# One decode step, attention beside a gated MLP: the MLP's output weights are dealt out anew over the DMA engines, and two products keep their weight loads

## The chip, the core and the metric

The kernel runs on one core of a Trainium2 chip. The metric is the device time of one execution in microseconds (us); the median over several runs is compared. Before the change it is 663.55 us, the median of three runs (663.48, 663.55 and 664.41).

The core has a matrix engine (PE in the profile, with its weight loads shown as PEld), three other compute engines (DVE, ACT, POOL), a queue engine that issues most transfers (SP), and sixteen DMA engines that move data from memory (HBM) into the on-chip buffer. A transfer is issued once and is then cut into packets, each of which one of the sixteen DMA engines carries out.

## The reference

For four sequences, one new token each, with `x` of 4 x 640 normalised to `xn`, the output is `x + A(xn) + B(xn)`.

```python
# A: attention over a cache of 4096 keys, 32 heads of 128
q = xn @ wq
p = softmax(q . k_cache * 128**-0.5)        # k_cache: 4 x 32 x 4096 x 128
A = (p . v_cache) @ wo                      # v_cache: 4 x 32 x 4096 x 128

# B: gated MLP, Fh = 864
z = gelu(xn @ w_in)                         # w_in: 640 x 1728
z1, z2 = z[:, :864], layernorm(z[:, 864:])
B = (z1 * (w_sp * z2 + b_sp)) @ w_out       # w_out: 864 x 640
```

All inputs are bf16. The two caches are 134 MB each; everything else together is about 15 MB. So nearly all of the time is spent in reading.

## The kernel before

**Attention.** The 128 pairs of a sequence and a head are cut into 16 units, each of one sequence and eight heads. A unit has 8 MB of keys and 8 MB of values. The order of the loads is the list `seq`: keys of units 0 to 3, then values of unit 0, keys of unit 4, values of unit 1, and so on (K0 K1 K2 K3 V0 K4 V1 K5 ... V15). Every load is written as 128 rows of 64 KB (some are cut in two), so each DMA engine carries eight packets of 64 KB per unit. The buffer `kv` has five slots of half a unit; the table `place` says which two slots a unit takes, and a load can be issued only when the last reader of those slots is done. SP issues all of these loads in order (L181), one step ahead of the compute loop at the end of the kernel.

For keys, DVE transposes blocks of a unit into `w_words` (L425, eight blocks per unit), and PE multiplies them by the query into the scores `S` (L436). After every fourth unit comes a softmax (L443 to L500), then PE multiplies probabilities and values into `O` (L509). The first four units of keys are done before the first values, so the values V1 can only be loaded once K0 to K3 are transposed, the first softmax is done, and half of V0 is multiplied.

**The MLP** runs in the first 45 us, while the first keys are on their way. Its product z (L338 to L343) is made in pieces that match the layout of `w_out`, so that after a transpose each row of z stands on the partition where the matching row of `w_out` is. `w_out` has 864 rows of 1280 bytes. The first 384 (`FA` = 3 per partition) go into slot 2 of `kv`, spread over all partitions and so over all DMA engines, 24 rows on each: two transfers, L126 (two rows per partition) and L127 (one row). The other 480 rows go into `w_rest`, a view of `w_words`, on only some partitions, by the table `PC`. Each entry (p0, p1, n, k) puts n rows on each of the partitions p0 to p1, and k is the outermost size of the transfer, which decides how many DMA engines take part:

| piece | issued by | partitions | rows on each | engines (k) | rows per engine |
|---|---|---|---|---|---|
| 0 | SP | 20 | 10 | 5 | 40 |
| 1 | SP | 12 | 12 | 3 | 48 |
| 2 | POOL | 8 | 17 | 2 | 68 |

A small transfer `walk` (L141) goes ahead of piece 2 on POOL's queue. `w_rest` has room for `FR` = 17 chunks and is cleared by one DVE memset first (L128); unused rows stay zero. The product with `w_out` then runs over `FC` = 20 chunks in two halves (L403), 40 matmuls, into the accumulator `proj`. `w_words` is reused by the key transposes right after.

**Queries.** `q4` (L301) is made of 40 matmuls: two halves, five chunks of the contraction, four column groups of PE. Each matmul call loads its weights (`xnT`, 32 columns) anew.

**The end.** The last transfers are `wo` of groups 1, 2 and 3 (L189), the last one cut into four (chunks 0 to 3, 4 and 5, 6, 7), so that PE can follow the landing closely (L552). A short chain of DVE operations (L600, L604, L615) and the output transfer (L618) follow.

Of the kernel before, what the change touches and what calls it, by code (L numbers as in the profile page):

```python
# [16 lines left out]
def kernel(  # L17
# [19 lines left out]
    nc = tc.nc  # L37
    P = 128
    B, Sq, D = A_x.shape
    _, H, Sk, Dh = A_k_cache.shape  # L40
    assert Sq == 1 and B == 4 and Dh == P and D % P == 0
    DC = D // P
    HG = 8
# [8 lines left out]
    NG = H // HG  # L52
# [2 lines left out]
    F2 = B_w_in.shape[1]  # L55
    Fh = F2 // 2
    FA = 3
    FR = 17
    nf = FA * P

    PC = ((0, 20, 10, 5), (32, 44, 12, 3), (60, 68, 17, 2))
    f_at = [nf]
    for p0, p1, n, _ in PC:
        f_at.append(f_at[-1] + (p1 - p0) * n)
    assert Fh == f_at[-1]
    FC = FA + FR
    NOUT = A_wo.shape[1]
# [12 lines left out]
    ps_m = ctx.enter_context(tc.tile_pool(name="ps_m", bufs=2, space=bass.MemoryType.PSUM))  # L80
    ps_j = ctx.enter_context(tc.tile_pool(name="ps_j", bufs=1, space=bass.MemoryType.PSUM))
    ps_l = ctx.enter_context(tc.tile_pool(name="ps_l", bufs=1, space=bass.MemoryType.PSUM))

    misc_ctr = [0]

    def misc_ps(shape, dtype):
        misc_ctr[0] += 1
        return ps_m.tile(shape, dtype, tag="misc", name=f"misc{misc_ctr[0]}")
# [5 lines left out]
    n_p = (2 * TC + 1) * 16  # L94
    w_words = const.tile([P, max(2 * NKT + n_p, FR * NOUT // 2)], F32, name="w_words")
    kT_t = w_words[:, 0:2 * NKT].rearrange("p (i n) -> p i n", i=2)
    pT_t = w_words[:, 2 * NKT:2 * NKT + n_p].bitcast(BF16).rearrange("p (j r) -> p j r", r=32)

    def at_slot(i, n, off=0):
        return kv[:, i * SL + off:i * SL + off + n]  # L100
# [17 lines left out]
    wq = at_slot(0, n_q).rearrange("p (c n) -> p c n", c=DC)  # L118
# [4 lines left out]

    w_out = at_slot(2, FA * NOUT, n_in).rearrange("p (c n) -> p c n", c=FA)

    nc.sync.dma_start(out=w_out[:, 0:2], in_=B_w_out[0:2 * P, :].rearrange("(p c) n -> p c n", p=P))  # L126
    nc.sync.dma_start(out=w_out[:, 2:3], in_=B_w_out[2 * P:nf, :].rearrange("(p c) n -> p c n", p=P))  # L127
    nc.vector.memset(w_words[:, 0:FR * NOUT // 2], 0.0)  # L128
    w_rest = w_words[:, 0:FR * NOUT // 2].bitcast(BF16).rearrange("p (c n) -> p c n", c=FR)

    def load_piece(eng, t):
        p0, p1, n, k = PC[t]
        return eng.dma_start(out=w_rest[p0:p1, 0:n].rearrange("p c n -> p (c n)"),
                             in_=B_w_out[f_at[t]:f_at[t + 1], :].rearrange("(r i c) n -> i r (c n)", i=k, c=n))
# [85 lines left out]
    xnT = const.tile([P, DC, 32], BF16)  # L220
# [43 lines left out]
    for q in range(4):  # L264
        nc.gpsimd.tensor_copy(out=SelE[32 * q:32 * q + 32, :, q % 2, :],
                              in_=b8[32 * q:32 * q + 32, 8:8 + HP, None].to_broadcast((32, HP, P // HG)))
# [10 lines left out]
                          in_=ident_f[:].rearrange("p (q x c) -> p q x c", q=2, c=C2))  # L277
# [12 lines left out]
    for hf in range(NH):  # L290
        nc.tensor.matmul(proj[0:32, 0:NO2], lhsT=ident_bf[:XR, 1 - hf:33 - hf],
                         rhs=x_bf[:, hf * NO2:(hf + 1) * NO2], start=(hf == 0), stop=False)
# [1 line left out]


    q4_ps = ps_s.tile([P, HG * Dh], F32, tag="S", name="q4")
    for hf in range(2):
        for c in range(DC):
            for j in range(NG):
                n0 = j * HG * Dh + hf * 512  # L300
                nc.tensor.matmul(q4_ps[32 * j:32 * j + 32, hf * 512:hf * 512 + 512], lhsT=xnT[:, c, :],  # L301
                                 rhs=wq[:, c, n0:n0 + 512], start=(c == 0), stop=(c == DC - 1))

    q4 = at_slot(0, 2 * HG * Dh, n_q + 8 * D).rearrange("p (i n) -> p i n", i=2)
    q4_in = q4_ps[:].rearrange("p (h a j w) -> p h a w j", h=HG, a=2, w=2)
# [11 lines left out]
    w_z = w_in.rearrange("p c (a f) -> p c a f", a=2)  # L317
    z_ps = misc_ps([P, 2, FA, 32], F32)
    zr_ps = misc_ps([P, 2, 256], F32)


    z_in = [[], [], [], []]
    for t, (p0, p1, n, k) in enumerate(PC):
        src = w_z[:, :, :, f_at[t]:f_at[t + 1]]
        for q in range(p0 // 32, (p1 - 1) // 32 + 1):
# [5 lines left out]
                src_q = src  # L331
            z_in[q].append((t, x0 - 32 * q, x1 - 32 * q, src_q))
    z_of = [[sum((x1 - x0) * PC[t][2] for t, x0, x1, _ in z[:m]) for m in range(len(z) + 1)] for z in z_in]
    w_z2 = w_z[:, :, :, 0:2 * P].rearrange("p c a (q j i) -> p c q a i j", q=4, j=32)
    w_z1 = w_z[:, :, :, 2 * P:nf].rearrange("p c a (q j) -> p c q a j", q=4)
    for c in range(DC):
        for q in range(4):
            nc.tensor.matmul(z_ps[32 * q:32 * q + 32, :, 0:2], lhsT=xnT[:, c, :], rhs=w_z2[:, c, q], start=(c == 0), stop=False)  # L338
            nc.tensor.matmul(z_ps[32 * q:32 * q + 32, :, 2], lhsT=xnT[:, c, :], rhs=w_z1[:, c, q], start=False,
                             stop=(c == DC - 1))  # L340
        for q in range(4):
            for m, (_, _, _, src) in enumerate(z_in[q]):
                nc.tensor.matmul(zr_ps[32 * q:32 * q + 32, :, z_of[q][m]:z_of[q][m + 1]], lhsT=xnT[:, c, :], rhs=src[:, c],  # L343
                                 start=(c == 0 and m == 0), stop=(c == DC - 1 and m == len(z_in[q]) - 1))
    z_f = at_slot(2, 2 * 3 * NB, z_at).bitcast(F32).rearrange("p (a n) -> p a n", a=3)
    z_b = at_slot(2, 2 * NB, z_at + 6 * NB).rearrange("p (a n) -> p a n", a=2)
    zT = z_f[:, 0:2, :].rearrange("p a (i j) -> p a i j", j=32)
# [2 lines left out]
    for q in range(4):  # L350
        rows = slice(32 * q, 32 * q + 32)
        for m, (t, x0, x1, _) in enumerate(z_in[q]):
            p0, p1, n, k = PC[t]
            z = zr_ps[rows, :, z_of[q][m]:z_of[q][m + 1]]
# [3 lines left out]
            else:  # L358
                for a in range(2):
                    nc.scalar.activation(out=dst[:, a].rearrange("p c (i r) -> p c i r", i=k),  # L360
                                         in_=z[:, a].rearrange("p (r i c) -> p c i r", i=k, c=n), func=ACT.Gelu_apprx_tanh)
# [36 lines left out]
    for f0 in range(0, FC, 4):  # L398
        for hf in range(NH):
            for fc in range(f0, min(f0 + 4, FC)):  # L400
# [3 lines left out]
                                 rhs=(w_out[:, fc] if fc < FA else w_rest[:, fc - FA])[:, hf * NO2:(hf + 1) * NO2],  # L404
                                 start=(fc == 1 and hf == 0), stop=False)
# [190 lines left out]
    for c, hf in ((0, 0), (1, 0), (0, 1), (1, 1), (2, 0), (2, 1)):  # L596
        p = min(c, 1)
# [9 lines left out]
    for c in range(3, HG):  # L607
        for hf in range(NH):
            for k in range(2):
                n0 = hf * NO2 + k * NQ  # L610
# [36 lines left out]
```

## Time and profile before

| what | before |
|---|---|
| time, median of three runs | 663.55 us |
| span of the profiled execution | 661.8 us |
| bytes read | 282.25 MB, 426 GB/s over the span |
| DMA engines busy | 90% or more in 39 of the 40 slices of the span |
| PE, DVE, ACT, POOL busy | 286.8, 377.1, 74.0, 70.1 us |
| share of the last chain that is DMA | 75% |

The span runs from the first to the last instruction of the one execution that was profiled. The profiled execution's own time is this span and what lies around it (the start and the end of the program); the median of the timed runs is 1.75 us longer than the span. DMA queue q1 carries what SP issues, q10 what ACT issues, q0 what POOL issues; q8 and q14, which the profile calls "instruction", carry the engines' own programs. A line of the chain of waits or of the timeline begins with the start and the duration in us.

Besides these views, the trace records every DMA packet with its start, duration, size and queue. It does not say which of the sixteen engines carried it. But the packets follow each other so closely (the next starts 3 to 4 ns before the last one ends) that they fall apart into sixteen chains, and each chain can be followed from the first load to the last. The sizes tell which chain is which: 12,800 bytes are ten rows of `w_out` (piece 0), 15,360 bytes twelve rows (piece 1), 21,760 bytes seventeen rows (piece 2).

### The profile page before, as it was taken

Reading aid. Unit: us, or ns where it says so; the run is one execution under the profiler, and the core shown is the slowest. Engines: PE = TensorE matmul, PEld = TensorE weight load, DVE = VectorE, ACT = ScalarE, POOL = GpSimd, SP = SyncE. Lnnn points to the kernel's source line nnn. Section 1 sums busy time; section 2 is a strip of 40 time slices with the busy share of each in tenths; the row PEclk is TensorE's granted clock in tenths of the full one; section 3 lists DMA queues with packets and bytes.
Section 4 is the critical chain, followed back from the end, with each engine's and each line's share of the span. In section 5 each row is a group of like instructions: output and inputs, shape, how many; then the busy total and the mean of one; then the engine's idle time right before and its main releaser. Section 6 shows DMA issues by size and latency. Waiting matters only on the chain.

```text
span 661.8 us, 5507 instructions
## 1 busy us (share of the span) xinstructions
PE 286.8 (43%) x2291; PEld 107.4 (16%) x2291; DVE 377.1 (57%) x307; ACT 74.0 (11%) x143; POOL 70.1 (11%) x138
## 2 busy tenths in 40 slices
PE   0336555446052456234426065642607245541236
PEld 0221111112011122111102022210202112120113
DVE  5329989766191759718346196764619175971112
ACT  0300000340100000330200000070100000042200
POOL 4620000030200000130300000030110000002300
PEclk9868788669578596676858587665857768766678
DMA  9999999999999999999999999999999999999997
GB/s 370 457 429 428 427 442 437 440 421 428 421 440 433 440 415 446 425 437 436 437 432 432 429 418 437 446 433 440 425 420 436 437 436 417 456 420 437 419 420 289
DMA packets 7132, 282.60 MB, mean 427 GB/s; under 512 B 913, under 2 KB 1308, under 8 KB 1692
## 3 DMA queue, kind: packets, MB, share of 16 engines
q1 hardware_dynamic: 6968, 282.07, 98.9%
q8 instruction: 18, 0.29, 0.2%
q0 software_dynamic: 112, 0.18, 0.1%
q14 instruction: 6, 0.05, 0.0%
q10 hardware_dynamic: 28, 0.01, 0.0%
HBM read 282.25 MB, written 0.01 MB: 426 GB/s over the span
## 4 chain that ended last, share of the span: by engine, by line
DMA 75%; DVE 11%; issue 11%; PE 2%; DVEq 0%; SPq 0%
DMA kv<-in_A_k_cache_dram 59%; DVE w_words L425 11%; DMA kv<-in_A_v_cache_dram 10%; DMA kv<-in_A_wo_dram 4%; DMA kv<-in_A_wq_dram 3%; PE O L509 2%; PE S L436 0%; PE proj L552 0%; DVE o_q L604 0%; DVE o L600 0%; DVEq L425 0%; SPq L189 0%; DVE o_bf L615 0%; SPq L181 0%; PE last L552 0%
## 5 line engine op out<-in xcount | busy, mean ns | idle before, releaser
L425 DVE STREAM_TRANSPOSE w_words<-kv 128x2048 f32<-128x2048 f32 x128 | 282.8, 2275 | 124.8 <-DMA kv<-in_A_k_cache_dram 124.8
L436 PE MATMUL S<-w_words,QZ 128*32 128x512 bf16 x1024 | 186.1, 496 | 258.3 <-DVE w_words L425 258.3
L436 PEld LDWEIGHTS <-QZ 128*32 128x32 bf16 x1024 | 59.7, 110 | 382.9 <-issue 319.5
L509 PE MATMUL O<-kv,Zb 128*32 128x512 bf16 x1024 | 75.0, 458 | 57.4 <-DMA kv<-in_A_v_cache_dram 50.8
L473 ACT ACTIVATE Zb<-w_words,MkE 32x128 bf16<-32x128 bf16 x120 | 61.0, 508 | 117.9 <-PE O L509 104.2
L518 DVE TENSOR_TENSOR om<-O,Mk 128x512 f32<-128x512 f32 x15 | 10.4, 692 | 94.6 <-PE O L509 94.6
L471 POOL TENSOR_SCALAR Zb<-w_words,MkE 32x128 bf16<-32x128 bf16 x60 | 43.1, 718 | 139.3 <-PE O L509 126.9
L509 PEld LDWEIGHTS <-Zb 128*32 128x32 bf16 x1024 | 34.0, 113 | 98.4 <-issue 70.3
L485 ACT ACTIVATE p_bf<-S,negmax 128x1024 bf16<-128x1024 f32 x4 | 4.5, 1114 | 401.8 <-DVE negmax L453 401.8
L469 DVE TENSOR_SCALAR Zb<-w_words,MkE 32x128 bf16<-32x128 bf16 x76 | 24.7, 325 | 2.3
L411 POOL COPY QZ<-qT 32x32 bf16<-32x32 bf16 x16 | 5.0, 315 | 186.4 <-PE S L436 185.9
L519 DVE TENSOR_REDUCE R<-om 128x128 f32<-128x512 f32 x15 | 15.3, 1020 | 0.5
L496 POOL TENSOR_SCALAR rs<-MkB,rowsum 128x4 f32<-128x4 f32 x4 | 1.2, 296 | 112.4 <-ACT p_bf L485 112.4
L491 DVE STREAM_TRANSPOSE w_words<-p_bf 128x1024 bf16<-128x1024 bf16 (+1 forms) x8 | 9.6, 1241 | 5.9 <-ACT p_bf L485 4.1
L542 POOL MEMSET oT<- 128x66 bf16 x4 | 0.5, 146 | 96.5 <-PE proj L552 96.5
L443 DVE TENSOR_REDUCE m<-S 128x1 f32<-128x1024 f32 x4 | 4.9, 1224 | 6.1 <-PE S L436 6.1
L521 DVE TENSOR_SCALAR R<-O,Mk 128x128 f32<-128x128 f32 x1 | 0.4, 351 | 14.0 <-PE O L509 14.0
L531 PE MATMUL misc<-R,SelX 128*128 128x512 f32 x8 | 4.5, 644 | 7.2 <-DVE R L519 5.5
L301 PE MATMUL q<-kv,xnT 128*32 128x512 bf16 x40 | 4.3, 617 | 6.4 <-DVE xnT L222 6.4
L498 PE MATMUL misc<-rs,SelE 128*128 128x4 f32 x8 | 2.4, 365 | 10.4 <-POOL rs L496 10.4
L128 DVE MEMSET w_words<- 128x5440 f32 x1 | 4.6, 4592 | 1.9 <-issue 1.9
L534 DVE TENSOR_TENSOR om<-misc,h 128x512 f32<-128x512 f32 x4 | 2.8, 692 | 4.9 <-PE misc L531 4.9
(107 smaller groups left out, 88.2 us busy)
## 6 DMA issues: line engine op xcount, KB each, us to landing
kv<-in_A_k_cache_dram SPq DMA_DIRECT2D x8, 4096.0 KB, 30.2
kv<-in_A_v_cache_dram SPq DMA_DIRECT2D x1, 6144.0 KB
kv<-in_A_wq_dram SPq DMA_DIRECT2D x1, 5120.0 KB, 16.8
kv<-in_A_wo_dram SPq DMA_DIRECT2D x3, 1280.0 KB
kv<-in_B_w_in_dram SPq DMA_DIRECT2D x1, 2160.0 KB, 22.3
kv<-in_A_v_cache_dram SPq DMA_DIRECT2D x1, 2048.0 KB
kv<-in_A_wo_dram SPq DMA_DIRECT2D x1, 640.0 KB, 23.6
kv<-in_B_w_out_dram SPq DMA_DIRECT2D x1, 320.0 KB
```

The source lines that it names most:

```text
L128: nc.vector.memset(w_words[:, 0:FR * NOUT // 2], 0.0)
L411: nc.gpsimd.tensor_copy(out=QZ[r0:r0 + 32, :, :, :, 8 + 8 * hp], in_=qT[32 * g:32 * g + 32, NE * hp:NE * hp + NE].rearrange("p e a b -> p ...
L425: nc.vector.transpose(kT.rearrange("p (t r) -> p t r", r=32), kw)
L436: nc.tensor.matmul(S_ps[32 * q:32 * q + 32, i], lhsT=QZ[:, b, 2 * kh + w, e, w0:w0 + 32], rhs=kb[:, i, :, e, :, w], start=(b == 0 and k < ...
L443: nc.vector.tensor_reduce(out=m1[:], in_=S_ps[:].rearrange("p i t m -> p (i t m)"), axis=AX.X, op=ALU.max)
L469: nc.vector.tensor_scalar(out=dst, in0=src, scalar1=mk, scalar2=None, op0=ALU.mult)
L471: nc.gpsimd.tensor_scalar(out=dst, in0=src, scalar1=mk, scalar2=None, op0=ALU.mult)
L473: nc.scalar.activation(out=dst, in_=src, func=ACT.Copy, scale=mk)
L491: nc.vector.transpose(pT_t[:, j0:j1, :], blocks)
L509: nc.tensor.matmul(O_ps[32 * q:32 * q + 32, :, :], lhsT=Zb[b % 2][:, w].rearrange("p h c -> p (h c)"), rhs=vv[:, w * 4 * Dh:(w + 1) * 4 * ...
L518: nc.vector.tensor_tensor(out=om4[:], in0=O_ps[:], in1=Mk4[:, :, None].to_broadcast((P, 4, Dh)), op=ALU.mult)
L519: nc.vector.tensor_reduce(out=R, in_=om4[:].rearrange("p c d -> p d c"), axis=AX.X, op=ALU.add)
```

## The change

- `w_out`, the first 384 rows: one transfer instead of two (three rows, 3840 bytes, per partition). Still 24 rows on each engine.
- `w_out`, the other 480 rows: piece 0 has 9 instead of 10 rows on its 20 partitions, over 5 engines (36 rows each). Piece 1 has 9 rows on 20 partitions instead of 12 on 12, over 5 engines instead of 3 (36 each). Piece 2 has 15 instead of 17 rows on its 8 partitions, over 2 engines (60 each). So five engines carry 72 rows each, where three carried 88 and two 40; two carry 60 where they carried 68.
- `FR` is 15 instead of 17, so the MLP has 18 chunks instead of 20: the memset, the passes over z and the product with `w_out` get shorter by a tenth or so.
- q: the contraction chunks are the outer loop; for each, four weight loads are written out (`load_w`), and both halves' matmuls use them (`mm_held`, a matmul without a weight load). 20 weight loads instead of 40, the same 40 matmuls, in a section that the scheduler keeps together.
- z: for each chunk four weight loads instead of twelve, and the first 384 columns in one matmul per column group instead of two: 20 weight loads and 40 matmuls instead of 60 and 60, again in one section.

```diff
-    FR = 17
+    FR = 15
-    PC = ((0, 20, 10, 5), (32, 44, 12, 3), (60, 68, 17, 2))
+    PC = ((0, 20, 9, 5), (32, 52, 9, 5), (60, 68, 15, 2))
...
+    def load_w(lhsT, q):
+        nc.tensor.ldweights(lhsT, tile_position=(0, 32 * q))
+
+    def mm_held(out, lhsT, rhs, start, stop, q):
+        nc.tensor.add_instruction(mybir.InstMatmult(
+            name=nc.get_next_instruction_name(), engine=mybir.EngineType.PE,
+            ins=[nc.tensor.lower_ap(rhs), nc.tensor.lower_ap(lhsT, for_matmul_weights=True)],
+            outs=[nc.tensor.lower_ap(out, opt=True)], start_tensor_calc=start, stop_tensor_calc=stop,
+            tile_size=(P, 32), tile_position=(0, 32 * q), ldweights=False))
...
-    nc.sync.dma_start(out=w_out[:, 0:2], in_=B_w_out[0:2 * P, :].rearrange("(p c) n -> p c n", p=P))
-    nc.sync.dma_start(out=w_out[:, 2:3], in_=B_w_out[2 * P:nf, :].rearrange("(p c) n -> p c n", p=P))
+    nc.sync.dma_start(out=w_out, in_=B_w_out[0:nf, :].rearrange("(p c) n -> p c n", p=P))
...
-    for hf in range(2):
+    with tc.tile_critical():
         for c in range(DC):
             for j in range(NG):
-                n0 = j * HG * Dh + hf * 512
-                nc.tensor.matmul(q4_ps[32 * j:32 * j + 32, hf * 512:hf * 512 + 512], lhsT=xnT[:, c, :],
-                                 rhs=wq[:, c, n0:n0 + 512], start=(c == 0), stop=(c == DC - 1))
+                load_w(xnT[:, c, :], j)
+            for hf in range(2):
+                for j in range(NG):
+                    n0 = j * HG * Dh + hf * 512
+                    mm_held(q4_ps[32 * j:32 * j + 32, hf * 512:hf * 512 + 512], xnT[:, c, :], wq[:, c, n0:n0 + 512],
+                            c == 0, c == DC - 1, j)
...
-    w_z2 = w_z[:, :, :, 0:2 * P].rearrange("p c a (q j i) -> p c q a i j", q=4, j=32)
-    w_z1 = w_z[:, :, :, 2 * P:nf].rearrange("p c a (q j) -> p c q a j", q=4)
-    for c in range(DC):
-        for q in range(4):
-            nc.tensor.matmul(z_ps[32 * q:32 * q + 32, :, 0:2], lhsT=xnT[:, c, :], rhs=w_z2[:, c, q], start=(c == 0), stop=False)
-            nc.tensor.matmul(z_ps[32 * q:32 * q + 32, :, 2], lhsT=xnT[:, c, :], rhs=w_z1[:, c, q], start=False,
-                             stop=(c == DC - 1))
-        for q in range(4):
-            for m, (_, _, _, src) in enumerate(z_in[q]):
-                nc.tensor.matmul(zr_ps[32 * q:32 * q + 32, :, z_of[q][m]:z_of[q][m + 1]], lhsT=xnT[:, c, :], rhs=src[:, c],
-                                 start=(c == 0 and m == 0), stop=(c == DC - 1 and m == len(z_in[q]) - 1))
+    w_za = w_z[:, :, :, 0:nf].rearrange("p c a (q j i) -> p c q a i j", q=4, j=32)
+    with tc.tile_critical():
+        for c in range(DC):
+            for q in range(4):
+                load_w(xnT[:, c, :], q)
+            for q in range(4):
+                mm_held(z_ps[32 * q:32 * q + 32], xnT[:, c, :], w_za[:, c, q], c == 0, c == DC - 1, q)
+            for q in range(4):
+                for m, (_, _, _, src) in enumerate(z_in[q]):
+                    mm_held(zr_ps[32 * q:32 * q + 32, :, z_of[q][m]:z_of[q][m + 1]], xnT[:, c, :], src[:, c],
+                            c == 0 and m == 0, c == DC - 1 and m == len(z_in[q]) - 1, q)
```

## The prediction

> **What bounds the kernel now.** I read the page's DMA rows first, then the chain of waits, then the timeline around the first keys and the end, then the packet records engine by engine.
>
> ```profile
> span 661.8 us, 5507 instructions
> ...
> DMA  9999999999999999999999999999999999999997
> ...
> q1 hardware_dynamic: 6968, 282.07, 98.9%
> q8 instruction: 18, 0.29, 0.2%
> ...
> q14 instruction: 6, 0.05, 0.0%
> ...
> DMA 75%; DVE 11%; issue 11%; PE 2%; DVEq 0%; SPq 0%
> ```
>
> The sixteen DMA engines are busy from start to end; nothing that a compute engine saves counts unless it lets a transfer land earlier. Queues q8 and q14 look like nothing: 24 packets. They turn out to matter.
>
> ```profile
> 17.55 27.97 DMA kv<-in_A_k_cache_dram
> 45.74 2.37 DVE w_words L425 x2
> 54.76 29.47 DMA kv<-in_A_k_cache_dram
> 84.42 2.32 DVE w_words L425
> ...
> 110.88 31.48 DMA kv<-in_A_k_cache_dram
> ...
> 633.41 23.56 DMA kv<-in_A_wo_dram
> 657.02 0.44 PE proj L552 x4
> ...
> 659.03 0.32 DVE o_bf L615
> ```
>
> The chain in order of time: K0 lands at 45.52, K2 at 84.23, and the end follows the last `wo` landings. A transfer has landed when the slowest of the sixteen engines is done with it, so the question is which engine is last.
>
> The packet records answer it. Followed as sixteen chains, every engine runs without a pause from 1.6 us to the end, with one exception at 137 us. When each has finished its last data, and why (large fetch: a 16 KB packet on q8; small fetch: 8 KB on q14):
>
> | engines, by rows of `w_out` beyond the common 24 | fetches | done at, us |
> |---|---|---|
> | three with 88 | one small, one small, none | 657.74, 658.11, 657.27 |
> | two with 40 | one small; three small | 655.61; 657.90 |
> | two with 68 | none | 656.13, 656.49 |
> | one with 0 | none | 653.92 |
> | eight with 0 | two or three large each | 656.01 to 657.85 |
>
> A large fetch sets its engine back by 1.55 us, a small one by 0.7 to 1.0 (the lag of the chain against the engine without any, before and after the fetch). The large ones go round the same eight engines, one per some 258 PE instructions: PE's program. The three small ones at 88.2, 278.7 and 470.8 us all fall on the same chain, one of the two with 40 rows, about 128 DVE instructions apart: DVE's program (inferred). So the engine that feeds DVE's program starts 2.3 us ahead of an engine with 88 rows and has used that up by 471 us.
>
> The exception: V1 is issued at 134.90, and the first engines run out of K4 at 136.97.
>
> ```profile
> 110.88 0.33 SPq L181 DMA_DIRECT2D kv<-in_A_k_cache_dram  x1
> 134.90 0.33 SPq L181 DMA_DIRECT2D kv<-in_A_v_cache_dram  x1
> ```
>
> Five of the eight PE-program engines lose there, four of them 1.0 to 2.0 us, besides one large fetch at 137.2. For every other load the first engine is at least 4.8 us from running dry when it is issued.
>
> **The change part by part.** Prices of rows: a 15,360-byte packet takes 573 ns and one of 12,800 bytes 479, so a row (1280 bytes) is 47 ns; nine rows are 479 - 47 = 432 ns, fifteen are 808 - 94 = 714 (seventeen took 808), three are 102 + 47 = 149.
>
> *Rows on five engines.* From 88 to 72: before 4 x 479 + 4 x 573 = 4.21 us, after 8 x 432 = 3.46, so -0.75. From 40 to 72: before 4 x 479 = 1.92, after 3.46, so +1.54. From 68 to 60: 4 x (714 - 808) = -0.38.
>
> *One transfer for the first 384 rows.* Per engine 8 x 102 + 8 x 55 + one 9 ns semaphore packet before, 8 x 149 after; with 4 ns of overlap per packet -0.04 us on every engine. A rule speaks for far more: the Trainium skill, "DMA: Bandwidth & Descriptors", section "Anatomy of one DMA", gives each transfer a fixed cost of about 2 us, mostly waiting for completion; by it the time would drop by 2.0. The records do not agree: behind the second load's semaphore packet the next load's first packet starts 6 ns later.
>
> *The end.* Adding these to the table: the 88-row engines finish at 656.95, 657.32, 656.48; the lighter 40-row engine at 655.61 + 1.50 = 657.11; the one with DVE's fetches at 657.90 + 1.50 = 659.40; the others move by -0.04 to -0.42 or gain from the next point. Last before was 658.11, last after 659.40: +1.29, or +1.26 with the overlaps of the four added packets and the measured sums (+1.48 net for that engine). The four pieces of the last `wo` all land that much later, and the tail behind them (landing at 656.97, PE, L600, L604, L615 until 659.35, output) is the same. Bounds: if the fetch packets cost that engine their bare 316 to 333 ns instead of 1 us, 2.0 less (no gain is excluded); if its first `w_out` packets run like the slowest first packets of `wq` (2.99 against 1.51 us), 1.5 more. I take +1.26, since the same chain is recorded from end to end.
>
> *K0 and K2 land earlier.* Last on both is an 88-row engine (its K2 done at 83.77; the DVE-fetch engine 80.97, after the change 82.4). So both land 0.8 us earlier, DVE, which is busy without a break from 84.42 through K2 and K3, runs 0.8 earlier, and V1 is issued at 134.1. That gives the PE-program engines up to 0.8 of their 1 to 2 us back. They were done at 657.85 at the latest, so this is off the path: nothing.
>
> *Weight loads and matmuls.* q: 20 loads fewer at a mean of 141 ns. They lie under the 40 matmuls, which take 4.31 us together; q feeds `qT` and K1's issue at 25.10, and no engine reaches K1 before 40.2, 15 us later. z: 20 matmuls and 40 loads fewer out of a block of 1.5 us. MLP: the POOL passes (1.25, 2.51, 0.87, 1.53 us) and the 4.5 us of L403 shrink by a tenth, about 1 us. The order by chunk makes both halves of q ready together; its copies wait for both already. The section that is kept together could hold PE back; between nothing and the length of the block, 4.3 us for q.
>
> ```profile
> 37.38 0.84 DVE L390 STREAM_TRANSPOSE kv<-kv 128x640 bf16<-128x640 bf16 x1 [5.32 <-POOL kv L389]
> ...
> 39.06 4.06 PE L403 MATMUL proj<-w_words,kv 128*8 128x320 bf16 x33
> ...
> 45.74 17.66 DVE L425 STREAM_TRANSPOSE w_words<-kv 128x2048 f32<-128x2048 f32 x8 [7.52 <-DMA kv<-in_A_k_cache_dram]
> ```
>
> Cover: the first key transpose overwrites `w_words`, so it waits for K0 and for L403. L403 ends at 43.3, K0's transpose starts at 45.74, after the change 44.9: 1.6 us of cover, and the MLP itself gets about 1 us shorter. Nothing. The memset (4.59 us, now 4.05) lets SP issue pieces 0 and 1 at 6.0 instead of 6.55; the engines reach them at 20.9. Nothing. With one transfer fewer ahead, K0's issue, which waited 9.2 us for `wq` until 17.55, may come up to 9 us earlier; the engines reach K0 at 21. Nothing.
>
> *Fewer PE instructions.* 20 + 60 + 8 = 88 fewer: each large fetch comes 88 instructions later, and the last, at 656.0, falls behind the end of the program. That spares one engine about 1 us that ended at 657.11. Nothing.
>
> Sum: 663.55 + 1.26 = 664.8, +0.19%. It is made on the profiled execution, whose span of 661.8 is 1.75 below the median of the timed runs; I take that difference as unchanged.
>
> **The rivals.**
>
> 1. *DVE's fetches do not ride on one of the five engines any more, or cost less, and the change does what its row counts say (not slower).* For it: that the stream is DVE's is inferred. Against: all three fetches and the rows are on one recorded chain. The last engine is then one with three large fetches, 657.59 - 0.04 = 657.55, against 658.11: 663.0. It decides if the lag of the DVE-fetch engine grows by less than 0.2 us, some five rows.
> 2. *The MLP is late.* A section that holds PE pushes L403 past 44.9, and with it the key chain and V1's issue. For it: V1's slack is the only thin one. Each further microsecond costs the five dry engines one. The latest of them (657.85) passes 659.40 when V1 comes 1.5 us later than before, that is when the MLP ends 4 us late (2.4 of cover before the change); a 5 us delay gives 665.8.
> 3. *A transfer has a start cost on each engine,* as the first packets of `wq` had (2.1 to 2.3 instead of 1.51 us): one transfer less gives 0.7 back everywhere: 664.1. Against: the 6 ns above.
>
> **How the numbers follow.** About 0.2% (1.33 us) is what a measurement of this kernel can tell from no change; the forecast lies just inside it, at 664.8 against 664.88. Forecast 0.76, with a range of its own of 664.4 to 665.3 (large fetches and the dry spell vary; one of three runs before was 0.9 above the others), 0.40 of it within the bound and 0.36 above. Rival 1 0.11 (of it 0.03 faster by more than 0.2%, should the dry engines and a fetch both gain), rival 2 0.06, rival 3 0.04, something unnamed that makes it faster 0.03. Together: faster 0.06, same 0.52, slower 0.42. The range 662.9 to 665.8 takes in rivals 1 and 3 and most of rival 2.
>
> **What would show it.** In the packet records: 11,520-byte packets, eight on each of five engines; the engine with the three 8 KB fetches done last, near 659.4, more than a microsecond behind the next. In the chain: K0's first transpose at about 44.9, K2's at 83.6, V1 issued near 134.1, L615 at about 660.3, span near 663.1. Wrong if that engine isn't last, if the fetches are elsewhere, or if the first transpose follows L403 instead of K0.

## The result, and the profile after

| what | before | after |
|---|---|---|
| time, median | 663.51 us | 686.37 us |
| ratio after to before (95% interval) | | 1.0343 (1.0331 to 1.0355) |
| span of the profiled execution | 661.8 us | 684.4 us |
| forecast | | 664.8 (662.9 to 665.8) |

The change costs 22.9 us, 3.4%. The forecast was 21.6 us too low, and the result lies far outside its range.

The page of the kernel after:

```profile
span 684.4 us, 5450 instructions
...
DMA  9936799999999999999999999999999999999996
GB/s 371 460 161 246 307 429 427 433 445 448 438 433 426 429 426 418 453 430 429 426 437 430 437 438 414 449 437 430 429 434 433 434 437 413 450 429 434 428 411 283
...
q1 hardware_dynamic: 6834, 282.09, 95.8%
...
DMA 68%; PE 9%; issue 7%; DVE 5%; POOL 1%; ACT 0%; SPq 0%; DVEq 0%; POOLq 0%; ACTq 0%
```

Before, every slice of the DMA row but the last was 9. Now the third to the fifth slice (34 to 86 us) read 3, 6, 7, and the bytes per second fall to 161 there. From the sixth slice on the row is as it was. The whole loss happens in the first 86 us: V1, issued at 157.96 instead of 134.90, is 23.1 us late, and the span is 22.6 us longer.

What SP waited for in those 86 us tells which transfer was late. First the longest wait of SP's queue before K1 (line, what was waited for, total us, times, longest) and the issue of K1, before and after, then the timeline of SP's issues in the kernel after (start, us; a line may group several issues):

```profile
SPq L181 <- POOL qT L312: 7.1, 1, 7.1
25.10 0.34 SPq L181 DMA_DIRECT2D kv<-in_A_k_cache_dram  x1
```

```profile
SPq L190 <- PEq L347: 49.2, 1, 49.2
57.45 0.33 SPq L190 DMA_DIRECT2D kv<-in_A_k_cache_dram  x1
```

```profile
7.63 92.29 SPq L190 DMA_DIRECT2D kv<-in_A_k_cache_dram  x5
117.13 0.33 SPq L190 DMA_DIRECT2D kv<-in_A_v_cache_dram  x1
134.68 0.33 SPq L190 DMA_DIRECT2D kv<-in_A_k_cache_dram  x1
157.96 0.33 SPq L190 DMA_DIRECT2D kv<-in_A_v_cache_dram  x1
```

SP issued K0 at 7.63 us and then stood 49.2 us before K1, which went out at 57.45. It waited for PE's queue at L347: the end of the second section, the one for z. Before the change K1 waited last for the query (`qT`) and was issued at 25.10. In the packet records all sixteen engines are done with K0 between 40.2 and 44.1 us and stand idle until 58.4 to 59.2, 16.6 us on average. They run dry again at 78.4 to 80.1, until 83.1 to 83.8, 4.6 us on average, because K2 is late too. V1, at 157.96, then comes in time: everything behind the second dry spell is moved as a block.

So why did the section end so late? The timeline of PE, first of the kernel before and then of the kernel after (start, us, instruction, in brackets the idle time before it and what ended it):

```profile
17.76 4.31 PE L301 MATMUL q<-kv,xnT 128*32 128x512 bf16 x40 [6.40 <-DVE xnT L222]
```

```profile
45.78 4.45 PE L88 MATMUL q<-kv,xnT 128*32 128x512 bf16 x40 [34.22 <-issue]
54.17 2.98 PE L88 MATMUL misc<-kv,xnT 128*32 128x192 bf16 x40 [3.94 <-POOL qT L324]
```

The same 40 matmuls take as long as before (4.45 against 4.31 us), but they start 28.0 us later. PE was idle for 34.22 us, and the view puts that down to "issue", a word for a wait that it can't name. PE's own semaphore records name it. The entry of the first section, L306, holds one record that waits for two transfers: the semaphore of `w_in` comes at 23.57, and that of K0 at 44.49. K0's last packet is done at 44.06. q was waiting for **keys that it does not read**.

The list of instructions as built shows the same (it isn't a profile, and is shortened here); DMAHW0 is the completion lane of K0's transfer:

```
after:     L306 NoOp  [waits DMAHW3, DMAHW1, DMAHW4, DMAHW0, DMAHW5, DVE, Pool]
after:     L190 DMACopy kv<-in_A_k_cache (K1)  [waits DMAHW1, PE_sequencer, DMAHW3, PE, Pool]
before:    K1's issue waits for Pool (qT) and lanes, not for PE_sequencer
```

`wq`, `w_in`, the first rows of `w_out` and K0 all lie in one buffer, `kv`, in different slots. Outside a section a matmul waits for the slot it reads (q started at 17.76 before, while K0 was on its way). The section waits once, at its entry, for the buffer; and a load into the buffer that comes later in the program waits for the section's end.

### The profile page after: what moved, and what is told of

It is laid out like the page before. It is cut to its first block, busy times and chain, and to the rows that moved or that the text cites. A ratio compares the mean times of both kernels' runs of the same rounds, so it can differ in the third digit from the quotient of the medians.

```text
span 684.4 us, 5450 instructions
## 1 busy us (share of the span) xinstructions
PE 284.4 (42%) x2267; PEld 106.5 (16%) x2227; DVE 376.3 (55%) x307; ACT 73.9 (11%) x143; POOL 69.4 (10%) x138
## 4 chain that ended last, share of the span: by engine, by line
DMA 68%; PE 9%; issue 7%; DVE 5%; POOL 1%; ACT 0%; SPq 0%; DVEq 0%; POOLq 0%; ACTq 0%
DMA kv<-in_A_v_cache_dram 61%; PE O L521 8%; DVE w_words L437 5%; DMA kv<-in_A_k_cache_dram 4%; DMA kv<-in_A_wo_dram 3%; PE proj L415 0%; POOL kv L399 0%; PE S L448 0%; POOL kv L401 0%; ACT L361 0%; POOL kv L384 0%; ACT kv L372 0%; POOL kv L400 0%; DVE kv L402 0%; DVE st_in L385 0%
## 5 line engine op out<-in xcount | busy, mean ns | idle before, releaser
L448 PE MATMUL S<-w_words,QZ 128*32 128x512 bf16 x1024 | 179.8, 482 | 251.6 <-DVE w_words L437 251.6
L448 PEld LDWEIGHTS <-QZ 128*32 128x32 bf16 x1024 | 58.4, 108 | 371.7 <-issue 307.9
L521 PE MATMUL O<-kv,Zb 128*32 128x512 bf16 x1024 | 76.9, 468 | 59.2 <-DMA kv<-in_A_v_cache_dram 56.1
L531 DVE TENSOR_REDUCE R<-om 128x128 f32<-128x512 f32 x15 | 15.3, 1020 | 0.5
L85 PEld LDWEIGHTS <-xnT 128*32 128x32 bf16 x40 | 2.0, 131 | 43.4 <-issue 43.0
```

The lines of the kernel that those rows point to most:

```text
L448: nc.tensor.matmul(S_ps[32 * q:32 * q + 32, i], lhsT=QZ[:, b, 2 * kh + w, e, w0:w0 + 32], rhs=kb[:, i, :, e, :, w], start=(b == 0 and k < ...
L521: nc.tensor.matmul(O_ps[32 * q:32 * q + 32, :, :], lhsT=Zb[b % 2][:, w].rearrange("p h c -> p (h c)"), rhs=vv[:, w * 4 * Dh:(w + 1) * 4 * ...
L531: nc.vector.tensor_reduce(out=R, in_=om4[:].rearrange("p c d -> p d c"), axis=AX.X, op=ALU.add)
```

## The experiments

**The theories.** *A:* a section waits for every transfer asked for so far into the buffers that it touches, K0 among them, and holds every later load into them until it ends. The loss is that wait. *B:* the sections or the held weight loads cost PE time of their own, or slow the matmuls. *C:* the rows, the single transfer or K0 asked for early are a large part of the loss.

### The rows without the sections

Everything of the change is kept, except that q and z are ordinary matmuls again and no section is left.

```diff
-    with tc.tile_critical():
-        for c in range(DC):
+    for hf in range(2):
+        for c in range(DC):
...
-                load_w(xnT[:, c, :], j)
...
-                    mm_held(q4_ps[...], xnT[:, c, :], wq[...], c == 0, c == DC - 1, j)
+                nc.tensor.matmul(q4_ps[...], lhsT=xnT[:, c, :], rhs=wq[...], start=(c == 0), stop=(c == DC - 1))
... (the same for z)
```

> The changed kernel with both sections and the held weight loads taken out: every matmul loads its own weights, the rows of w_out, the one transfer and the 18 chunks stay as changed. Theory A (a section waits for every earlier transfer into the buffer kv, so for K0, and every later transfer into kv waits for the section's end): without sections q starts near 17.8 us again, K1 is issued near 25, and what is left is the ledger of the prediction, the engine with DVE's fetches last: 664.8 us (+1.26). Theory B (the sections or held matmuls cost by themselves, without K0's part in it): also back near 664. Theory C (the new rows, or K0's issue at 7.6 instead of 17.5 us, are the cause): stays near 686.

Measured: 664.95 us (664.75 to 665.31, 11 runs) against 663.51 (15 runs) for the kernel before in the same job, ratio 1.0021 (1.0012 to 1.0030). That is the forecast of 664.8 within 0.15 us, so the rows, the single transfer and the early K0 make up 1.4 of the 22.9 us, and the sections with their held loads the other 21.4. C falls.

The packet records, engine by engine, as in the prediction's table (done with the last data, us):

| engines | forecast | measured |
|---|---|---|
| 72 rows and the three small fetches | 659.40 | 659.39 |
| the other four with 72 rows | 656.48 to 657.32 | 656.55 to 657.21 |
| two with 60 rows | 655.71, 656.07 | 655.84, 655.91 |
| one with 0 | 653.88 | 654.00 |
| eight with 0 and large fetches | up to 657.8 | 655.87 to 657.70 |

The end of this kernel, in its timeline:

```profile
658.29 0.44 PE L558 MATMUL proj<-kv,oT 128*8 128x320 bf16 x4 [0.26 <-DMA kv<-in_A_wo_dram]
...
660.30 0.32 DVE L621 TENSOR_TENSOR o_bf<-last,o_q 64x160 bf16<-64x160 f32 x1
```

The last piece of `wo` has landed when PE starts at 658.29, and the last DVE operation starts at 660.30, where the prediction had "about 660.3" (before: 659.03). The engine with three 8 KB fetches is last, 1.7 us behind the next.

### One section at a time

In the first kernel only q keeps its section and z is ordinary; in the second it is the other way round.

```diff
 # q_section: z without a section
-    with tc.tile_critical():
-        for c in range(DC):
-            for q in range(4):
-                load_w(xnT[:, c, :], q)
+    for c in range(DC):
...
-                mm_held(z_ps[...], xnT[:, c, :], w_za[:, c, q], c == 0, c == DC - 1, q)
+            nc.tensor.matmul(z_ps[...], lhsT=xnT[:, c, :], rhs=w_za[:, c, q], start=(c == 0), stop=(c == DC - 1))
```

> The changed kernel with the section around q alone; z is made of ordinary matmuls. Theory A: the section still waits for K0's landing, q starts near 45.8 us, the query is ready near 53.4, K1 is issued there instead of at 25 and the DMA engines stand still from 40 to 44 until about 55; the first key transpose waits for the MLP until about 61, and K2 is issued before the engines run dry: about 677 us. Theory B: the start is set by the section's own length, a few microseconds at most: under 668. Theory C: 686.

> The changed kernel with the section around z alone; q is made of ordinary matmuls. Theory A: q starts near 17.8 us and the query is ready near 25, so nothing of q holds K1 back; yet K1 is issued only when the z section ends, near 49, because K1 goes into kv after it; the MLP ends near 65, K2 is issued near 74: about 677.5 us. Theory B: K1 is issued near 25, and the time is under 668. Theory C: 686.

Measured, one run each: 679.89 us with q's section alone, 677.62 with z's. The waits of SP's queue in the first 100 us, the first matmuls of z, and PE in the window of z (window, us, PE busy, granted clock, DMA share, GB/s), q's section alone:

```profile
SPq L190 <- PEq L306: 41.7, 1, 41.7
...
SPq L190 <- POOL qT L324: 2.9, 1, 2.9
```

```profile
23.23 0.35 PE L349 MATMUL misc<-kv,xnT 128*32 128x192 bf16 x4 [11.99 <-DMA kv<-in_B_w_in_dram]
...
23.24:26.23 2.99, 2.98 (x40) 1.00 1.33 575
```

and the timeline and the same waits with z's section alone:

```profile
18.38 3.69 PE L310 MATMUL q<-kv,xnT 128*32 128x512 bf16 x40 [6.76 <-DMA kv<-in_A_wq_dram]
...
45.80 2.89 PE L88 MATMUL misc<-kv,xnT 128*32 128x192 bf16 x40 [23.74 <-issue]
```

```profile
SPq L190 <- PEq L344: 30.5, 1, 30.5
```

Either section alone stands until K0 has landed: q at 45.52 in one, z at 45.80 in the other, while the product without a section runs at its old place (18.38 for q, 23.23 for z). K1 goes out behind the section, at 52.79 and 48.90. Either one costs most of the loss, 16.4 and 14.1 us over the kernel before, because both wait for the same landing; in the kernel after, the second section only adds its own chain behind the first (q's copies and transposes, then z). The time with q's section was 2.9 us above the 677 expected: I had thought that K2 would go out before the engines ran dry a second time, but they were dry for 3.1 us on average there.

### K0 asked for behind the sections

The issue of K0 is moved behind the second section in the program; nothing else is changed. Now the section has no key load to wait for.

```diff
-    load_unit(seq[0])
...
     (z's section)
+    load_unit(seq[0])
```

> The changed kernel with one line moved: K0's load is written after the z section instead of before q. Theory A: the first section then waits for wq, w_in and w_out alone (landed near 24.8 us), q starts near 25.6, the z section ends near 36.7, K0 is issued there and the DMA engines stand still from 21 to 25 until about 38; no second dry spell: about 679 us, that is 7 less than the changed kernel although K0 is asked for 29 us later. Theory B: the sections cost the same as before and K0 comes later on top: 686 or more.

Measured: 681.42 us, one run. PE's timeline and the waits of SP's queue:

```profile
25.72 4.45 PE L88 MATMUL q<-kv,xnT 128*32 128x512 bf16 x40 [14.11 <-issue]
...
34.11 2.95 PE L88 MATMUL misc<-kv,xnT 128*32 128x192 bf16 x40 [3.94 <-POOL qT L323]
```

```profile
SPq L190 <- PEq L346: 29.6, 1, 29.6
```

Both sections are still there with the same work inside, and q starts 20.1 us earlier. So it was K0 that they waited for, and not something inside them (against B). What is left of the wait, until 25.72 instead of 17.8, is the other loads into `kv`: by PE's semaphore records the entry passes `w_in` at 23.33 and the first rows of `w_out` at 24.48, and further entry steps of the section take the other 1.2 us. The kernel is 5.0 us faster than the kernel after (7 were expected; nothing here shows what the other 2 are) although K0 itself is asked for 29.6 us later, at 37.23, and the engines are dry from 20.9 to 24.8 until 38.2 to 38.8. This edit takes the wait away but puts the dry spell elsewhere; the next one has neither.

### K0 in another buffer

The buffer is cut in two: slots 0 to 2 (where `wq`, `w_in` and `w_out` lie) and slots 3 and 4 (where K0 goes). Five units that lie over the cut are loaded in two halves. Both sections, the held loads and all rows are kept. The control has the same cut and halves, without sections and with ordinary matmuls.

```diff
-    kv = const.tile([P, 5 * SL], BF16)
+    kv = const.tile([P, 3 * SL], BF16, name="kv")
+    kv_hi = const.tile([P, 2 * SL], BF16, name="kv_hi")
...
+        if i >= 3:
+            return kv_hi[:, (i - 3) * SL + off:(i - 3) * SL + off + n]
         return kv[:, i * SL + off:i * SL + off + n]
...
+    for item in place:
+        if place[item] == (2, 3) and item not in cuts:
+            cuts[item] = (0, T // 2, T)
```

> The changed kernel with both sections, but the big buffer kv is cut into two tiles: slots 0 to 2 (wq, w_in, the first rows of w_out, later keys and values) and slots 3 and 4, where K0 goes. Loads that lie over the cut are issued in two halves. Nothing else is changed. Theory A (a section waits for every transfer asked for so far into the tiles it touches, whole tiles): K0 is in another tile now, so the first section starts when wq, w_in and w_out have landed, q at about 25.6 us as in k0_after_sections (25.72) instead of 45.8; z ends near 37, K1 is issued near 37.2, before the engines run out of K0 at 40.2, so the dry spell at K1 is gone; the MLP ends near 53 and not 73, the key transposes start there and not at 45.7, DVE is some 4.5 us behind at K2, V1 is issued near 139.4, and the engines are dry for some 2 us at 137. Time 664.5 to 668, I take 667, so 18 to 22 us under the changed kernel. Theory B (sections and held weight loads cost PE time themselves, or slow the matmuls): stays at 684 or above. Theory C (the rows, or K0 asked for early): stays at 686, since both are kept.

> The control for kv_split: the same two tiles and half loads, without sections and with ordinary matmuls. Theory A: as rows_only, 664.9 (664.2 to 666), q at about 18, first key transpose near 45, V1 issued at 133 or before. If the split itself costs (five more transfers), it shows here: more than 666.

Measured: 665.73 us (665.57 to 667.0, 4 runs; the views below are of the one that took 667.0), ratio to the kernel before 1.0037 (1.0023 to 1.0051); the control 665.34 (one run). PE's timeline, SP's waits and two lines of the chain and of SP's issues, all with sections and the cut:

```profile
25.70 4.45 PE L88 MATMUL q<-kv,xnT 128*32 128x512 bf16 x40 [14.51 <-issue]
34.09 2.98 PE L88 MATMUL misc<-kv,xnT 128*32 128x192 bf16 x40 [3.94 <-POOL qT L330]
```

```profile
SPq L196 <- PEq L353: 29.2, 1, 29.2
```

```profile
53.06 2.37 DVE w_words L443 x2
```

```profile
138.42 0.33 SPq L196 DMA_DIRECT2D kv<-in_A_v_cache_dram  x1
```

Apart from the cut and the five loads in halves, which the control has too, only the name of the buffer that K0 lands in has changed, and 20.6 of the 21.4 us of the sections are gone. The steps came where theory A had put them: q at 25.70 (25.6 expected), K1 issued at 37.36 (37.2), before the first engine runs out of K0 at 40.2, the key transposes from 53.06 (53), V1 at 138.42 (139.4). What is left is 0.4 us above the control's one run. In the packet records eight engines are dry for up to some 3 us around 138 to 140, before V1, and a few around 98, before V0, 1.0 us on average over all sixteen; the control has neither, so that is the likely source. B falls: two sections with their held loads cost next to nothing once K0 is out of their way.

In the built list the entry of the section has lost exactly one wait:

```
kv_split:  L312 NoOp  [waits DMAHW3, DMAHW4, DMAHW1, DMAHW5, DVE, Pool]
```

The six kernels side by side. The idle time of the engines is the mean over all sixteen, from the packet records, both dry spells together; the last column is the time above the kernel without sections.

| kernel | q starts | K1 issued | engines idle, us | V1 issued | time | above |
|---|---|---|---|---|---|---|
| without sections | 18.14 | 25.53 | 0 | 132.92 | 664.95 | |
| sections, cut buffer | 25.70 | 37.36 | 1.0 (before V0 and V1) | 138.42 | 665.73 | 0.8 |
| z's section | 18.38 | 48.90 | 12.8 | 148.83 | 677.62 | 12.7 |
| q's section | 45.52 | 52.79 | 15.3 | 152.04 | 679.89 | 14.9 |
| sections, K0 behind them | 25.72 | 37.78 | 15.8 (before K0) | 149.76 | 681.42 | 16.5 |
| after | 45.78 | 57.45 | 21.2 | 157.96 | 686.37 | 21.4 |

The time follows the idle time of the engines, in every row within 0.7 us, and not PE's delay: with the cut buffer q is 8 us late and K1 12 us, and that costs next to nothing, because the engines had K0 to read until 40.2.

### The sections with the old rows

The kernel after, with the rows and the 20 chunks of the kernel before.

```diff
-    FR = 15
+    FR = 17
-    PC = ((0, 20, 9, 5), (32, 52, 9, 5), (60, 68, 15, 2))
+    PC = ((0, 20, 10, 5), (32, 44, 12, 3), (60, 68, 17, 2))
```

> The changed kernel with both sections, but with the rows of the kernel before on the five and the two engines and 20 chunks. Theory A (the loss is the sections', and both dry spells align the engines anew, so that rows read before them do not count): 686 (685 to 688), q at about 45.8, K1 issued near 57.5. Theory C (the rows are a large part of the loss): 680 or less.

Measured: 687.01 us, one run; q at 46.65. With sections the new rows are not the slower ones. In the kernel after, the engines end K0 over a stretch of 3.9 us and start K1 within 0.8 us of each other, so what each had read of `w_out` before the dry spell no longer sets the end. What is left of the rows is when K0 lands, since the section waits for the slowest engine: K0's semaphore came at 45.35 with the old rows and at 44.49 with the new ones. What the rows cost (1.4 us) and what the sections cost do not add up.

### Other rows

On the kernel without sections, 36 rows for the engine with DVE's fetches and its neighbour, 80 for the other three of the five, 84 for the two that POOL feeds.

```diff
-    FR = 15
+    FR = 14
-    PC = ((0, 20, 9, 5), (32, 52, 9, 5), (60, 68, 15, 2))
+    PC = ((0, 20, 9, 5), (32, 44, 11, 3), (58, 70, 14, 2))
```

> Built on rows_only (no section, ordinary matmuls). The 480 rows of w_out beyond the common 24 are dealt anew from the packet records of rows_only: the two engines that had 40 rows before, of which one carries the three 8 KB fetches, get 36; the other three of the five get 80; the two fed by POOL get 84; 17 chunks in the MLP instead of 18. In rows_only the engine with the fetches was done last, at 659.39 us. Theory A (rows, by the ledger: 47 ns a row): that engine ends 36 x 0.047 = 1.70 us earlier, at 657.69; the three with 80 rows at 657.21 + 0.38 = 657.6 or before; the two with 84 at 655.9 + 1.13 = 657.0; last is then the engine with three 16 KB fetches, 657.70. That is 0.41 before the last of the kernel before (658.11): 663.1 us, 0.06% under it, and 1.8 under rows_only. Rival (the 1.4 us of rows_only have another source than the rows, such as 18 chunks or the single transfer): stays near 664.9.

Measured: 663.91 us (663.74 to 664.16, 11 runs) against 663.49 (15 runs), ratio 1.0005 (0.9996 to 1.0014): no difference from the kernel before, and 1.0 us below the rows of the change. The engine with the fetches is done at 657.71 (657.69 expected), the three with 80 rows at 657.31 to 657.55 (657.6 or before). Missed were the two with 84: 657.90 and 658.35, not 657.0. Their six POOL packets of 17,920 bytes take 0.67 us and more, 4.3 in all on one of them and 4.4 on the other, where four of 19,200 took 0.71 each, 2.8 in all; and two packets of `wq` between them took 1.87 us each instead of 1.51. So another engine is last now. Dealt ideally, by an estimate from these records, the bound is the engine with three large fetches (657.7 to 657.8 against 658.11 before), 0.05%, which can't be told from nothing here. No version beat the kernel before.

## Why the prediction was wrong, by its steps

- **The step that failed** is one sentence under weight loads and matmuls: "The section that is kept together could hold PE back; between nothing and the length of the block, 4.3 us for q." It held q back by 28.0 us. The bound took a section for a block of instructions that nothing may come between, as long as they take themselves. In this kernel it is also a wait at the entry for the whole of `kv`, and a wait of all later loads into `kv` for its exit; the runs with the section alone, with K0 moved and with the buffer cut show both.
- *"no engine reaches K1 before 40.2, 15 us later"* was right as a fact and is what made the cover look safe. The cover against a late K1 was 15 us; K1 came 32.4 us late (57.45 against 25.10).
- *K0's issue "may come up to 9 us earlier ... Nothing."* It came at 7.63, as said, and alone it cost nothing (rows without sections). K0's load stands ahead of q in the program, before the change as after it, so it is among what the section waits for at either issue time; that it was issued earlier is not part of the cause.
- *Rival 2* had the mechanism (a section that holds PE) and the wrong path and size. It followed the hold through the MLP to V1, one us for one, from a 4 us delay on. The first key transpose waited for the MLP (L415) until 73.13 instead of starting at 45.74, which is one of the signs that the prediction had named for being wrong, and V1 was issued at 157.96; but the engines were idle at K1 and K2, and had no dry spell at V1. It was given a chance of 0.06 with a price of 1 to 2 us, because the bound above was taken for its size. Rivals 1 and 3 fell: the fetches are on one of the five (659.39), and one transfer less gave no 0.7 us.
- *The rows, the single transfer, the shorter MLP*: right, shown without sections. +1.26 forecast, +1.44 measured; the engine that is last and its time to 0.01 us. The Trainium skill, "DMA: Bandwidth & Descriptors", section "Anatomy of one DMA — SWDGE (gpsimd) path", gives about 2.0 us as the fixed cost of a transfer that GpSimd issues; the prediction had it for every transfer, and the one that was saved is SP's. Taken over to it, the cost would have given 662.8 us for the kernel without sections; 664.95 was measured, so this run does not agree.
- *K0 and K2 earlier, V1 at 134.1*: right in kind (by its own line L403 ended at 43.1 and not 43.3, which changes nothing). First transpose at 45.11 (44.9 forecast), V1 at 132.92, 1.2 us earlier than forecast. The dry spell at 137 us is gone altogether, where a part of it had been forecast to stay; it was off the path, as said.
- *Weight loads: nothing.* Right for q: its 40 matmuls took 4.03 to 4.45 us with 20 loads and 3.69 to 4.46 with 40. z's 40 matmuls took 2.75 to 2.98 us with 20 loads, and with 40 loads 1.86 to 2.03 in three kernels but 2.99 in the one with q's section alone; before, with 60 of each, 1.57. So the held form saved nothing there, and the spread was hidden.

Could it have been seen? No row of the trace of before shows a section. But its price had an end that rows do show: everything in `kv` that was asked for by then. The last of it, K0, landed at 45.52 in the profile of before. A bound of "q may start as late as 45.5" therefore stood in the first line of the chain.

## What to carry to other kernels

Before a construct that orders work is priced at the length of that work, list the transfers into and out of every buffer that it touches, by buffer and not by slot, and take the last landing as its far bound: here that was the difference between 4 and 28 us. A load that stands ahead of such a construct in the program can be part of what it waits for, even when the work inside does not read it: here moving K0's load behind the sections took 20 us off q's start, though it only put the idle time elsewhere. Where several uses share one buffer, cutting it in two is a cheap way to learn whether a wait is real or only comes from the name.

## What the runs showed of the hardware

- After a dry spell the engines start together, and earlier differences in load between them no longer set the end: they ended K0 between 40.2 and 44.1 us and started K1 between 58.4 and 59.2. The old rows, 1.4 us better without sections, were not better with them (687.01, one run, against 686.37).
- In this kernel, whose engines are otherwise busy throughout, idle time of the engines is paid about one for one: 12.8, 15.3, 15.8 and 21.2 us idle on average cost 12.7, 14.9, 16.5 and 21.4 us.
- A DMA engine's lag by program fetches can be forecast closely: 659.39 against 659.40, and 657.71 against 657.69 with 36 rows instead of 72. The three 8 KB fetches came at 89.8, 277.8 and 472.3 us without sections and at 91.8, 278.5 and 470.6 with the rows dealt anew a second time, each time on the same chain of the five. Without sections a 16 KB fetch took 1.5 to 1.6 us from its engine and an 8 KB fetch 0.6 to 1.0, its own packet and the data packets beside it that it lengthened together.
- Fewer weight loads in a row did not shorten the products. q's 40 matmuls took 4.03 to 4.45 us with 20 loads and 3.69 to 4.46 with 40; z's took 2.75 to 2.98 us with 20 loads and 1.86 to 2.99 with 40. The granted clock does not sort z's times either (2.89 us at 0.54 with z's section alone, 2.98 at 1.00 in the kernel after). What does was not tried.
